# K^T of the attention heads by crossbar transpose instead of TensorE transposes, with changed loads and orders around it

## The chip, the cores and the metric

The kernel runs on one core of one Trainium2 chip. The metric is device time in microseconds (us) from the first to the last instruction of the program. The kernel before took 5017.94 us, the median of three runs (5016.48 to 5026.38).

## The reference

The kernel computes the forward output and eight gradients of a block of attention and a gated unit that are multiplied with each other:

```python
# x: 1 x 2048 x 576; 32 heads of 128; k_cache, v_cache: 1 x 32 x 2048 x 128; F = 4608
def _A_ref(x, k_cache, v_cache, wq, wo):          # attention on cached K and V
    q = (x @ wq) -> heads
    scores = einsum("bhqd,bhkd->bhqk", q, k_cache) * (128 ** -0.5)
    p = softmax(scores)
    return einsum("bhqk,bhkd->bhqd", p, v_cache) -> 2048 x 4096 @ wo
def _B_ref(x, w_gate, w_up, w_down):              # gated unit
    return (sigmoid(x @ w_gate) * (x @ w_up)) @ w_down

xn = layernorm(x)
s = _A_ref(xn, k_cache, v_cache, wq, wo)
g = silu(_B_ref(xn, w_gate, w_up, w_down))
out = x + s * g
# returned: out, and by jax.vjp with grad_out the gradients of
# x, k_cache, v_cache, wq, wo, w_gate, w_up, w_down
```

All tensors are bf16. No causal mask, no dropout: every head is a full 2048 x 2048 score matrix, forward and backward.

## The kernel before

The program goes through these stages, one after the other: LayerNorm, the gate and up products (with a guard that bounds the scores, so that the softmax needs no maximum); the down product; attention with its backward pass, head by head; then the output product with wo, the weight gradients of the gated unit, those of wq and wo, and the gradient of x.

**A head of attention** has two phases of 16 slots, one slot for each tile of 128 queries. In a slot of phase 1, `main1` makes 128 x 2048 scores in two halves, ACT applies Exp, and the slab `Pq` is transposed by a DMA transpose (`PT`). In a slot of phase 2, `main2` makes dP, turns the slab into dS in place, and has it transposed too (`dST`). Besides, TensorE works on units put into the slots: the products that read `PT` and `dST` five slots later (`tail1`, `tail2`, SKEW = 5), the K and V gradients that read the slabs as they are, and the preparation of the next head.

```python
def transpose_slab(hs, qt, name):
    T = wpt.tile([P, NT, P], bf, name=name, tag="PT")
    nc.sync.dma_start_transpose(T[:], hs.slabs[qt][:])
    return T

def s_half(hs, qt, hf):                            # reads QT and KT, both halves of the tile KQ
    ...
def main2(hs, qt, hf):
    ...                                            # dp: two matmuls of 128 x 512
    if (hf == NHF - 1) != (qt == 0 and NHF > 1 and hf in (0, NHF - 1)):
        nc.vector.scalar_tensor_tensor(Pq[:, hsl], dp[:], hs.negdelta[:, qt:qt + 1], Pq[:, hsl], op0=ALU.add, op1=ALU.mult)
    else:
        t = wt.tile([P, HW_], bf, name="t")
        nc.scalar.activation(t[:], dp[:], AF.Identity, bias=hs.negdelta[:, qt:qt + 1], scale=1.0)
        nc.vector.tensor_tensor(Pq[:, hsl], t[:], Pq[:, hsl], op=ALU.mult)
    if hf == NHF - 1:
        hs.dST[qt] = transpose_slab(hs, qt, "dST")
```

**K^T** is made from the loaded K, `Kn`, with 16 TensorE transposes into PSUM and two ACT copies out of it. For the first head this is done before attention begins, for each other head in phase 2 of the head before:

```python
def prep_kt(hs):
    KTv = hs.KT[:].rearrange("p (t q) -> p t q", q=P)
    pe_transpose_blocks(lambda j: hs.Kn[:, j, :], 0, NT, lambda g, n: KTv[:, g:g + n, :], "s")

def plan(h):
    ...                                            # pl: first slot of phase 2 of head h - 1
        for c in range(4):
            put(pl + q(c), 0, lambda c=c: load_k(hd(), c, 4))
        ...
        put(pl + q(skew + 3), NT * P, lambda: prep_kt(hd()))
```

The slots are given in program order; the framework's scheduler may place an instruction earlier on its engine.

**wo for the stage after attention** is loaded during the last head into buffers that it has finished with (`xnT`, `dsT`, a `Kn`, `Vn`, `dOn`), two heads' rows a load, each behind a small GpSimd copy that waits for a slab:

```python
def paced(slot, view, a, b):
    hs = heads[H - 1]
    nc.gpsimd.tensor_copy(view[0:1, a, 0:1], hs.slabs[slot % NT][0:1, 0:1])
    load_wo_rows(view, view_h0[id(view)], a, b)
```

In the same head SP also issues the first transposed loads of the attention output (`oT`) for that stage.

**LayerNorm turn.** In the first stage a row of x is normalised on ACT (`norm`), transposed on TensorE (`turn`) and copied out by ACT, one row per step between the ten matmuls of a gate/up step:

```python
def turn_step():
    if todo["turn"] and not (todo["norm"] and todo["norm"][0] <= todo["turn"][0] + 1):
        st = todo["turn"].pop(0)
        turn(st)
        return st
...                                                # one step:
    ready = turn_step()
    ...                                            # 5 matmuls g_ps, 5 matmuls u_ps
    put_T(ready, "s")                              # ACT copy
    nc.scalar.activation(a_row[:, cs], g_ps[:], AF.Sigmoid)
    nc.vector.tensor_tensor(h_row[:, cs], u_ps[:], a_row[:, cs], op=ALU.mult)
    ...
    ln_step(False)                                 # the next row's norm
```

Of the kernel before, what the change touches and what calls it, by code (L numbers as in the profile page):

```python
# [13 lines left out]
P = 128  # L14
# [52 lines left out]
def kernel(  # L67
# [164 lines left out]
    with tc.tile_pool(name="pa", bufs=1) as pa:  # L232
# [75 lines left out]
        with tc.tile_pool(name="a1w", bufs=1) as wp:  # L308
# [37 lines left out]
            with tc.tile_pool(name="a0", bufs=3) as sb0, tc.tile_pool(name="a0ps", bufs=2, space=PSUM) as ps0, \  # L346
# [68 lines left out]
                        norm(todo["norm"].pop(0))  # L415

                def turn_step():
                    if todo["turn"] and not (todo["norm"] and todo["norm"][0] <= todo["turn"][0] + 1):
                        st = todo["turn"].pop(0)
                        turn(st)  # L420
                        return st
# [168 lines left out]
    def attention(fast):  # L590
        with ExitStack() as es:
# [13 lines left out]
                    return ps_acc.tile([P, 4, P], f32, name="acc", tag="acc")  # L605
                return ps_acc.tile([P, 8, P], bf, name="acct", tag="acc")
            acc_box[0] = acc_alloc
            warm = stat.tile([P, 1], f32, name="warm")
            nc.scalar.activation(warm[:], eps_t[:], AF.Exp)

            def start_head(h):
                hs = heads_pre[h] if h == 0 else new_head(h)
# [83 lines left out]
            def main2(hs, qt, hf):  # L696
                Pq, hsl = hs.slabs[qt], slice(hf * HW_, (hf + 1) * HW_)
                dp = ps_big.tile([P, HW_], f32, name="dp", tag="big")
                for c in range(HW_ // CH):
                    nc.tensor.matmul(dp[:, c * CH:(c + 1) * CH], lhsT=hs.dOT[:, qt * P:(qt + 1) * P],  # L700
                                     rhs=hs.VT[:, hf * HW_ + c * CH: hf * HW_ + (c + 1) * CH], start=True, stop=True)
                if (hf == NHF - 1) != (qt == 0 and NHF > 1 and hf in (0, NHF - 1)):
                    nc.vector.scalar_tensor_tensor(Pq[:, hsl], dp[:], hs.negdelta[:, qt:qt + 1], Pq[:, hsl], op0=ALU.add, op1=ALU.mult)  # L703
                else:
                    t = wt.tile([P, HW_], bf, name="t")
                    nc.scalar.activation(t[:], dp[:], AF.Identity, bias=hs.negdelta[:, qt:qt + 1], scale=1.0)  # L706
                    nc.vector.tensor_tensor(Pq[:, hsl], t[:], Pq[:, hsl], op=ALU.mult)  # L707
                if hf == NHF - 1:
                    hs.dST[qt] = transpose_slab(hs, qt, "dST")

            def tail2(hs, qt, part):
                tail_part(hs, hs.dST[qt], hs.Kn, part)
# [69 lines left out]
            def plan(h):  # L782
                b1, b2 = 2 * NT * h, 2 * NT * h + NT
                hd = lambda: heads[h]
                pl = b2 - 2 * NT if h else None
                if h:
                    put(pl, 0, lambda: heads.__setitem__(h, start_head(h)))
                    for c in range(4):
                        put(pl + q(c), 0, lambda c=c: load_k(hd(), c, 4))
                        put(pl + q(skew + 3 + c), 0, lambda c=c: load_v(hd(), c, 4))  # L790
                    put(pl + q(4), 0, lambda: load_wo(hd()))
                    put(pl + q(5), 0, lambda: load_wq(hd()))
                    put(pl + q(skew + 3), NT * P, lambda: prep_kt(hd()))
                    put(pl + q(skew + 4), DT * P, lambda: prep_wot(hd()))
                    for sc in range(NSC):
                        put(pl + q(skew + 4 + 2 * sc), DT * CH, lambda sc=sc: prep_qt(hd(), sc))
                for qt in range(NT):
                    put(b1 + qt + skew, NT * P // 2, lambda qt=qt: tail1(hd(), qt, 0))
                    put(b1 + qt + skew, NT * P // 2, lambda qt=qt: tail1(hd(), qt, 1))
                for sc in range(NSC):  # L800
                    put(b1 + q(sc), DT * CH, lambda sc=sc: prep_dot(hd(), sc))
                    put(b1 + q(sc + 1), nb * P, lambda sc=sc: prep_don(hd(), sc))
                for qt in range(NT):
                    put(b1 + max(qt + 1, q(2 + qt // nb)), 0, lambda qt=qt: scale_don(hd(), qt))
                put(b1 + q(NSC + 2), NT * P, lambda: prep_vt(hd()))
                put(b1 + q(NTH + 2), NT * P, lambda: prep_qn(hd()))
                for qt in range(NT):
                    put(max(b1 + qt + 1, b1 + NT - 4 + qt // 2 if qt < NTH else b1 + NT + qt), 0, lambda qt=qt: scale_qn(hd(), qt))
                put(b2 + 1, 0, lambda: post1(hd()))
                parts = {}  # L810

                def first(key, rhs, lo, hi, eng, factor=1.0):
                    parts[key] = part_tile()
                    return Partial(hd(), lo, hi, rhs, parts[key], None, eng, factor)
                spread(b1 + NTH, lambda: first("v", hd().dOn, 0, NTH, "v"))
                spread(b2, lambda: Partial(hd(), NTH, NT, hd().dOn, parts["v"], out_3[0, h], None))
                spread(b2 + NTH, lambda: first("k", hd().Qn, 0, NTH, "s", SCALE))
                spread(b2 + NT, lambda: Partial(hd(), NTH, NT, hd().Qn, parts["k"], out_2[0, h], None, SCALE))
                for qt in range(NT):
                    put(b2 + qt + skew, NT * P // 2, lambda qt=qt: tail2(hd(), qt, 0))  # L820
                    put(b2 + qt + skew, NT * P // 2, lambda qt=qt: tail2(hd(), qt, 1))
# [2 lines left out]
            for h in range(H):  # L824
                plan(h)
            bl = 2 * NT * (H - 1) + NT
            dead_from = (5 - NT, 5 - NT, skew + 2, NTH + 2, -NT)
            free = [k for k in range(-NT, NT) if k < 3 - NT or (k > 3 - NT and k % 2)]
            free += [k for k in range(skew + 2, NT) if k % 2 == 0]

            def paced(slot, view, a, b):
                hs = heads[H - 1]
                nc.gpsimd.tensor_copy(view[0:1, a, 0:1], hs.slabs[slot % NT][0:1, 0:1])
                load_wo_rows(view, view_h0[id(view)], a, b)
            view_h0 = {}
            for view, h0, n, dead in sorted(wo_parts, key=lambda w: dead_from[w[3]]):
                view_h0[id(view)] = h0
                for k in range(0, n, 2):
                    at = min([f for f in free if f >= dead_from[dead]] or [NT - 1])
                    if at in free:  # L840
                        free.remove(at)
                    put(bl + at, 0, lambda at=at, view=view, k=k, n=n: paced(at, view, k, min(k + 2, n)))
            for st in range(min(2, NT)):
                put(bl + NT + skew * st, 0, lambda st=st: load_oT(oTs[st], st))
            slot = 0
# [32 lines left out]
    with late("pc") as pc, late("pcw") as pcw, late("pcf") as pcf, \  # L878
# [120 lines left out]
        dqb0 = ah0[:].rearrange("p a t f -> p (a t f)")[:, :NT * HG * P].rearrange("p (t c) -> p t c", c=HG * P)  # L999
        assert HG * P <= 2 * FB  # L1000

        def load_on(on_, hg):
            nc.gpsimd.dma_start(on_, rows_view(on2_d, hg * HG * P, HG * P))

        def load_dq(dq_, hg):
            nc.gpsimd.dma_start(dq_, rows_view(dq2_d, hg * HG * P, HG * P))

        with late("b1r", 2) as dblk, late("b1l") as ldp, late("b1t", 3) as tmpp, late("b1o", 2) as outp, \
# [5 lines left out]
            for fb in range(NFB):  # L1014
# [8 lines left out]
                    load_blk(nxt[:, 1, :, :], h_d, fb + 1)  # L1023
                du_blk = dblk.tile([P, NT, FB], bf, name="du_blk")
                dg_blk = dblk.tile([P, NT, FB], bf, name="dg_blk")
                if fb == NFB - 1:
                    if NFB % 2:
                        dqb0_late = True
                    else:
                        dqb0_late = False  # L1030
                        load_dq(dqb0, 0)
                for st in range(NT):
                    srows = slice(st * P, (st + 1) * P)
                    dh = ps.tile([P, FB], f32, name="dh")
# [10 lines left out]
                nc.gpsimd.dma_start(rows_view(dg_d, fb * FB, FB), dg_blk[:])  # L1045
                if fb == NFB - 1:
                    nc.gpsimd.dma_start(ds_all, rows_view(ds_d, 0, D))
                    load_on(onb0, 0)
                for fl in range(FB // P):
                    dwd = outp.tile([P, D], bf, name="dwd")  # L1050
                    accumulate(psa, h_blk, doB, slice(fl * P, (fl + 1) * P), dwd, "acc")
# [2 lines left out]
                for (blk_, out_, nm) in ((du_blk, out_7, "dwu"), (dg_blk, out_6, "dwg")):  # L1054
# [5 lines left out]
                        accumulate(psa, blk_, xn_all, lcols, dwT, "acc")  # L1060
                        nc.sync.dma_start_transpose(stg_[:, :, lcols], dwT[:])
                    store_T(out_, fcols, stg_)
            if dqb0_late:
                load_dq(dqb0, 0)
        pc2.release()

        pc3 = tc.alloc_tile_pool(name="pc3", bufs=1, reuse_waits="tile")
# [32 lines left out]
        with late("c2w") as wp, late("c2b") as blk, late("c2s", 2) as sb, late("c2ps", 4, space=PSUM) as ps:  # L1100
# [3 lines left out]
            for hg in range(NHG):  # L1104
                cols = slice(hg * HG * P, (hg + 1) * HG * P)
                onb, dqb = onqs[hg % 2]
                if hg + 1 < NHG:
                    load_on(onqs[(hg + 1) % 2][0], hg + 1)
                    load_dq(onqs[(hg + 1) % 2][1], hg + 1)
                dwq = dwqs[hg % 2]  # L1110
                for hl in range(HG):
                    h = hg * HG + hl
# [14 lines left out]
        with late("c4s", 2) as sb, late("c4cf") as chp, late("c4ps", 2, space=PSUM) as ps:  # L1127
# [10 lines left out]
            class Rows:  # L1138
# [24 lines left out]
                def finish(self):  # L1163
                    nj = len(ncs)
                    for sl in range(nsl):
                        st = self.sbi * nsl + sl
                        rows = slice(st * P, (st + 1) * P)
                        dxn = sb.tile([P, D], f32, name="dxn")
                        ca = sb.tile([P, nj], f32, name="ca")
                        cb = sb.tile([P, nj], f32, name="cb")  # L1170
                        junk = sb.tile([P, D], f32, name="junk")
                        for j, (n0, nn) in enumerate(ncs):
                            nc.scalar.activation(dxn[:, n0:n0 + nn], self.accs[sl][j][:, :nn], AF.Copy, accum_out=ca[:, j:j + 1])  # L1173
                            nc.vector.scalar_tensor_tensor(junk[:, n0:n0 + nn], self.accs[sl][j][:, :nn], 1.0, xn_all[:, st, n0:n0 + nn],  # L1174
                                                           op0=ALU.mult, op1=ALU.mult, accum_out=cb[:, j:j + 1])
                        cs = sb.tile([P, 2], f32, name="cs")
                        nc.vector.tensor_reduce(cs[:, 1:2], cb[:], axis=AX.X, op=ALU.add)
                        nc.vector.tensor_reduce(cs[:, 0:1], ca[:], axis=AX.X, op=ALU.add)
                        m12 = sb.tile([P, 2], f32, name="m12")
                        nc.vector.tensor_scalar(m12[:], cs[:], -1.0 / D, None, op0=ALU.mult)  # L1180
                        t = sb.tile([P, D], f32, name="t")
# [51 lines left out]
```

## Time and profile before

| what | before |
|---|---|
| device time, median of three | 5017.94 us |
| span of the profiled execution | 5024.2 us |
| TensorE matmul, busy | 4914.6 us |
| VectorE (DVE), busy | 2582.2 us |
| ScalarE (ACT), busy | 2575.9 us |
| attention, first to last slab transpose | 488.4 to 3605.9 us |
| slab transposes (PT and dST) | 512 + 512 |

A profile is one execution of the program. PE is TensorE's matmuls, PEld its weight loads, SP the engine that issues the DMA transposes, POOL (GpSimd) the one that issues most other transfers. A row of a group reads: line of the kernel, engine, operation, written tile <- read tiles, shape, count | busy us, mean ns of one | idle us of the engine just before them, and what ended most of that idle time. A matmul's mean is its pipelined duration, so the busy time over the count is what one costs in a row. A row of waits reads: who waited <- for whom: us in total, times, longest. The DMA share is the busy time of 16 DMA engines over the span; packets of different queues overlap, so it can exceed 1. In a row of the timeline the first two numbers are start and length in us, and the idle time before it stands in brackets.

### The profile page before, as it was taken

How to read it: one execution, taken by the hardware profiler on the slowest of the kernel's cores; microseconds unless marked ns; L12 is line 12 of the kernel's file. 1: busy time of each engine (PE TensorE's matmuls, PEld its weight loads, DVE VectorE, ACT ScalarE, POOL GpSimd, SP SyncE). 2: the span in 40 equal slices, each digit the busy share in tenths (PEclk: the TensorE clock that was granted, in tenths of full speed). 3: DMA queues.
4: the chain of work that ended last, by engine and by line, in shares of the span. 5: the costliest groups of instructions: out<-in, count | busy, mean ns of one | idle time of the engine just before them, and what ended most of it. 6: DMA issues, size and time to landing. Idle time of an engine off the chain costs nothing.

```text
span 5024.2 us, 128236 instructions
## 1 busy us (share of the span) xinstructions
PE 4914.6 (98%) x53584; PEld 3475.1 (69%) x54480; DVE 2582.2 (51%) x6721; ACT 2575.9 (51%) x4637; POOL 961.8 (19%) x1507
## 2 busy tenths in 40 slices
PE   9999999999999999999999999999889999999999
PEld 4445787787787788778778877877646666555554
DVE  4545666666666666666666666665425444200111
ACT  5422766766666676666667666666413333211000
POOL 3322111111111111111111111111222222211000
PEclk9999999999999999999999999999999999999999
DMA  7887999999999999999999999999996665797876
GB/s 260 273 206 167 211 213 205 206 215 212 202 214 216 201 212 208 214 208 209 215 202 213 206 213 210 209 215 203 209 196 206 195 189 183 223 264 178 171 140 121
DMA packets 2762803, 1031.39 MB, mean 205 GB/s; under 512 B 2665377, under 2 KB 2669602, under 8 KB 2762210
## 3 DMA queue, kind: packets, MB, share of 16 engines
q1 hardware_dynamic: 2659746, 699.38, 75.7%
q0 software_dynamic: 101856, 323.05, 20.0%
q8 instruction: 428, 7.01, 0.6%
q14 instruction: 165, 1.35, 0.1%
q10 hardware_dynamic: 608, 0.59, 0.0%
HBM read 175.31 MB, written 182.13 MB: 71 GB/s over the span
## 4 chain that ended last, share of the span: by engine, by line
PE 92%; DMA 3%; issue 3%; DVE 1%; ACT 0%; SPq 0%; POOL 0%; POOLq 0%; ACTq 0%; DVEq 0%
PE acc L737 18%; PE acc L677 18%; PE acc L975 13%; PE sp L630 8%; PE dp L700 7%; PE acc L1157 6%; PE acc L213 6%; PE u_ps L448 3%; PE g_ps L446 3%; PE dh L1036 3%; PE acc L531 3%; PE acct L146 2%; PE acc L945 2%; DMA dST<-Pq 1%; DMA xnT<-on_d 1%
## 5 line engine op out<-in xcount | busy, mean ns | idle before, releaser
L648 ACT ACTIVATE Pq<-sp 128x1024 bf16<-128x1024 f32 x1024 | 1048.1, 1024 | 309.7 <-PE sp L630 196.4
L737 PEld LDWEIGHTS <-Pq 128*128 128x128 bf16 x16384 | 1003.9, 98 | 244.3 <-issue 1.1
L703 DVE SCALAR_TENSOR_TENSOR Pq<-dp,negdelta,Pq 128x1024 bf16<-128x1024 f32 x512 | 655.3, 1280 | 37.7 <-PE acc L677 36.5
L706 ACT ACTIVATE t<-dp,negdelta 128x1024 bf16<-128x1024 f32 x512 | 568.1, 1116 | 178.4 <-PE dp L700 123.0
L677 PEld LDWEIGHTS <-PT 128*128 128x128 bf16 x8192 | 501.0, 98 | 128.6 <-DMA PT<-Pq 11.5
L677 PE MATMUL acc<-Vn,PT 128*128 128x128 bf16 x8192 | 547.4, 219 | 17.0 <-DMA PT<-Pq 10.1
L737 PE MATMUL acc<-dOn,Pq 128*128 128x128 bf16 x8192 | 552.3, 219 | 10.1
L677 PE MATMUL acc<-Kn,dST 128*128 128x128 bf16 x8192 | 551.3, 219 | 9.1 <-DMA dST<-Pq 5.5
L630 PE MATMUL sp<-KQ 128*128 128x512 bf16 x1762 | 547.1, 379 | 2.2 <-ACT Pq L648 2.1
L737 PE MATMUL acc<-Qn,Pq 128*128 128x128 bf16 x8192 | 540.6, 219 | 3.4
L700 PE MATMUL dp<-VT,dOT 128*128 128x512 bf16 x1728 | 540.8, 379 | 0.0
L707 DVE TENSOR_TENSOR Pq<-t,Pq 128x1024 bf16<-128x1024 bf16 x512 | 354.6, 693 | 359.7 <-ACT t L706 351.9
L677 PEld LDWEIGHTS <-dST 128*128 128x128 bf16 x8192 | 492.0, 98 | 68.2 <-DMA dST<-Pq 7.4
L718 ACT ACTIVATE dq_n<-acc,rsc 128x128 bf16<-128x128 f32 x512 | 188.4, 368 | 331.7 <-PE acc L677 329.4
L1174 DVE SCALAR_TENSOR_TENSOR junk<-acc,xn_all 128x512 f32<-128x512 f32 (+1 forms) x32 | 13.9, 453 | 635.6 <-ACT dxn L1173 635.6
L751 POOL DMA_DIRECT2D out_dram<-kvo x256 | 140.8, 550 | 999.7 <-DVE kvo L749 999.7
L671 POOL DMA_DIRECT2D on_d<-o_n x128 | 97.3, 760 | 721.4 <-DVE junk L689 374.8
L1038 DVE TENSOR_TENSOR du_blk<-dh,ah 128x256 bf16<-128x256 f32 x288 | 120.4, 419 | 195.5 <-PE dh L1036 193.4
L1173 ACT ACTIVATE dxn<-acc 128x512 f32<-128x512 f32 (+1 forms) x32 | 12.8, 407 | 396.7 <-PE acc L1157 389.2
L635 DVE TENSOR_REDUCE rs_all<-rsp 128x1 f32<-128x2 f32 x512 | 78.1, 153 | 255.7 <-ACT Pq L648 253.4
L50 DVE TENSOR_SCALAR o_n<-acc,rinv_all 128x128 bf16<-128x128 f32 x352 | 123.3, 350 | 161.5 <-PE acc L677 161.5
L648 ACT ACTIVATION_READ_ACCUMULATOR Pq<-sp 128x1 f32 x1024 | 200.5, 196 | 0.0
(213 smaller groups left out, 6977.0 us busy)
## 6 DMA issues: line engine op xcount, KB each, us to landing
out_dram<-kvo POOLq DMA_DIRECT2D x256, 128.0 KB, 4.2
ah<-a_d POOLq DMA_DIRECT2D x18, 1024.0 KB, 7.2
ah<-h_d POOLq DMA_DIRECT2D x18, 1024.0 KB, 9.4
du_d<-du_blk POOLq DMA_DIRECT2D x18, 1024.0 KB, 8.0
dg_d<-dg_blk POOLq DMA_DIRECT2D x18, 1024.0 KB, 9.7
h_d<-h_row POOLq DMA_DIRECT2D x64, 256.0 KB, 3.5
a_d<-a_row POOLq DMA_DIRECT2D x64, 256.0 KB, 3.7
x_all<-in_A_k_cache_dram SPq DMA_DIRECT2D x64, 256.0 KB, 3.8
```

Of the source, the lines that this page charges most:

```text
L213: nc.tensor.matmul(av[:, :CH], lhsT=w[:, i, :], rhs=srcT[:, i, cs], start=(i == 0), stop=(i == DT - 1))
L630: nc.tensor.matmul(sp[:, c * CH:(c + 1) * CH], lhsT=hs.QT[:, qt * P:(qt + 1) * P], rhs=hs.KT[:, hf * HW_ + c * CH: hf * HW_ + (c + 1) * CH ...
L648: nc.scalar.activation(Pq[:, hsl], sp[:], AF.Exp, scale=SCALE, accum_out=hs.rsp[:, hf:hf + 1])
L677: nc.tensor.matmul(hs.acc[:, 0, :], lhsT=T[:, kt, :], rhs=rhs[:, kt, :], start=(kt == 0), stop=(kt == NT - 1))
L700: nc.tensor.matmul(dp[:, c * CH:(c + 1) * CH], lhsT=hs.dOT[:, qt * P:(qt + 1) * P], rhs=hs.VT[:, hf * HW_ + c * CH: hf * HW_ + (c + 1) * C ...
L703: nc.vector.scalar_tensor_tensor(Pq[:, hsl], dp[:], hs.negdelta[:, qt:qt + 1], Pq[:, hsl], op0=ALU.add, op1=ALU.mult)
L706: nc.scalar.activation(t[:], dp[:], AF.Identity, bias=hs.negdelta[:, qt:qt + 1], scale=1.0)
L707: nc.vector.tensor_tensor(Pq[:, hsl], t[:], Pq[:, hsl], op=ALU.mult)
L718: nc.scalar.activation(hs.dq_n[:, qt % G4, :], hs.acc[:, 0, :], AF.Copy, scale=hs.rsc[:, qt:qt + 1])
L737: nc.tensor.matmul(self.tile[:, j, :], lhsT=self.slabs[qt][:, kt * P:(kt + 1) * P], rhs=self.rhs[:, qt, :], start=(qt == self.lo), stop=(q ...
L975: nc.tensor.matmul(accs[j][:, :nn], lhsT=lhs[:, st, cols], rhs=rhs[:, st, n0:n0 + nn], start=(st == 0), stop=(st == NT - 1))
L1157: nc.tensor.matmul(self.accs[sl][j][:, :nn], lhsT=ch[:, kk, sl * P:(sl + 1) * P], rhs=wT[:, k0 + kk, n0:n0 + nn], start=(self.k + kk == 0) ...
```

## The change

The main part: for all heads but the first, K^T comes from one DMA transpose of the loaded `Kn` straight into `KT`, on the queue that also carries the slab transposes. It is meant to take 16 transposes and two copies a head off TensorE and ACT.

```diff
+            def turn_nat(dst, src):
+                nc.sync.dma_start_transpose(dst[:].rearrange("p (t q) -> p t q", q=P), src[:].rearrange("p t d -> p (t d)"))
...
-                    put(pl + q(skew + 3), NT * P, lambda: prep_kt(hd()))
+                    put(pl + q(skew + 3), 0, lambda: turn_nat(hd().KT, hd().Kn))
```

With it come other differences. The wo rows of the last head are loaded up to four heads at a time, without the copies that hold them back:

```diff
-                for k in range(0, n, 2):
-                    at = min([f for f in free if f >= dead_from[dead]] or [NT - 1])
-                    if at in free:
-                        free.remove(at)
-                    put(bl + at, 0, lambda at=at, view=view, k=k, n=n: paced(at, view, k, min(k + 2, n)))
+                for k in range(0, n, 4):
+                    at = (1 + k // 4, q(skew + 1), q(skew + 2), q(skew + 4), q(skew + 5))[dead]
+                    put(bl + q(at), 0, lambda view=view, h0=h0, k=k, n=n: load_wo_rows(view, h0, k, min(k + 4, n)))
```

A row's turn in the first stage may follow on its own norm; the first dS slab of a head no longer takes DVE for its first half and ACT for its second; a dummy Exp at the start of attention is gone:

```diff
-                    if todo["turn"] and not (todo["norm"] and todo["norm"][0] <= todo["turn"][0] + 1):
+                    if todo["turn"] and not (todo["norm"] and todo["norm"][0] <= todo["turn"][0]):
...
-                if (hf == NHF - 1) != (qt == 0 and NHF > 1 and hf in (0, NHF - 1)):
+                if hf == NHF - 1:
...
-            warm = stat.tile([P, 1], f32, name="warm")
-            nc.scalar.activation(warm[:], eps_t[:], AF.Exp)
```

In the late stages, the dq rows of the first group of heads are loaded together with its on rows, after the gradients of the last block of the gated unit are stored, where before they were loaded ahead of that block's matmuls; and two small reduces at the end of each tile of dx become one:

```diff
-                        load_dq(dqb0, 0)
...
-                    load_on(onb0, 0)
+                    load_heads(onb0, dqb0, 0)
...
-                        nc.vector.tensor_reduce(cs[:, 1:2], cb[:], axis=AX.X, op=ALU.add)
-                        nc.vector.tensor_reduce(cs[:, 0:1], ca[:], axis=AX.X, op=ALU.add)
+                        nc.vector.tensor_reduce(cs[:], cc[:], axis=AX.X, op=ALU.add)
```

More of the change, by code (lines that the diff above doesn't have):

```diff
@@ L701, in main2 @@
                                      rhs=hs.VT[:, hf * HW_ + c * CH: hf * HW_ + (c + 1) * CH], start=True, stop=True)
-                if (hf == NHF - 1) != (qt == 0 and NHF > 1 and hf in (0, NHF - 1)):
+                if hf == NHF - 1:
                     nc.vector.scalar_tensor_tensor(Pq[:, hsl], dp[:], hs.negdelta[:, qt:qt + 1], Pq[:, hsl], op0=ALU.add, op1=ALU.mult)
+                    hs.dST[qt] = transpose_slab(hs, qt, "dST")
                 else:
@@ L707, in main2 @@
                     nc.vector.tensor_tensor(Pq[:, hsl], t[:], Pq[:, hsl], op=ALU.mult)
-                if hf == NHF - 1:
-                    hs.dST[qt] = transpose_slab(hs, qt, "dST")
             def tail2(hs, qt, part):
@@ L826, in attention @@
             bl = 2 * NT * (H - 1) + NT
[L827 to L837, printed above, removed]
-                for k in range(0, n, 2):
-                    at = min([f for f in free if f >= dead_from[dead]] or [NT - 1])
-                    if at in free:
-                        free.remove(at)
-                    put(bl + at, 0, lambda at=at, view=view, k=k, n=n: paced(at, view, k, min(k + 2, n)))
+            for view, h0, n, dead in wo_parts:
+                for k in range(0, n, 4):
+                    at = (1 + k // 4, q(skew + 1), q(skew + 2), q(skew + 4), q(skew + 5))[dead]
+                    put(bl + q(at), 0, lambda view=view, h0=h0, k=k, n=n: load_wo_rows(view, h0, k, min(k + 4, n)))
             for st in range(min(2, NT)):
@@ L1000, with load_heads @@
         assert HG * P <= 2 * FB
-        def load_on(on_, hg):
+        def load_heads(on_, dq_, hg):
             nc.gpsimd.dma_start(on_, rows_view(on2_d, hg * HG * P, HG * P))
-        def load_dq(dq_, hg):
             nc.gpsimd.dma_start(dq_, rows_view(dq2_d, hg * HG * P, HG * P))
@@ L1025 @@
                 dg_blk = dblk.tile([P, NT, FB], bf, name="dg_blk")
[L1026 to L1030, printed above, removed]
-                        load_dq(dqb0, 0)
                 for st in range(NT):
@@ L1062 @@
                     store_T(out_, fcols, stg_)
-            if dqb0_late:
-                load_dq(dqb0, 0)
         pc2.release()
@@ L1107 @@
                 if hg + 1 < NHG:
-                    load_on(onqs[(hg + 1) % 2][0], hg + 1)
-                    load_dq(onqs[(hg + 1) % 2][1], hg + 1)
+                    load_heads(*onqs[(hg + 1) % 2], hg + 1)
                 dwq = dwqs[hg % 2]
@@ L1168, in finish @@
                         dxn = sb.tile([P, D], f32, name="dxn")
-                        ca = sb.tile([P, nj], f32, name="ca")
-                        cb = sb.tile([P, nj], f32, name="cb")
+                        cc = sb.tile([P, 2, nj], f32, name="cc")
                         junk = sb.tile([P, D], f32, name="junk")
                         for j, (n0, nn) in enumerate(ncs):
-                            nc.scalar.activation(dxn[:, n0:n0 + nn], self.accs[sl][j][:, :nn], AF.Copy, accum_out=ca[:, j:j + 1])
+                            nc.scalar.activation(dxn[:, n0:n0 + nn], self.accs[sl][j][:, :nn], AF.Copy, accum_out=cc[:, 0, j:j + 1])
                             nc.vector.scalar_tensor_tensor(junk[:, n0:n0 + nn], self.accs[sl][j][:, :nn], 1.0, xn_all[:, st, n0:n0 + nn],
-                                                           op0=ALU.mult, op1=ALU.mult, accum_out=cb[:, j:j + 1])
+                                                           op0=ALU.mult, op1=ALU.mult, accum_out=cc[:, 1, j:j + 1])
                         cs = sb.tile([P, 2], f32, name="cs")
-                        nc.vector.tensor_reduce(cs[:, 1:2], cb[:], axis=AX.X, op=ALU.add)
-                        nc.vector.tensor_reduce(cs[:, 0:1], ca[:], axis=AX.X, op=ALU.add)
+                        nc.vector.tensor_reduce(cs[:], cc[:], axis=AX.X, op=ALU.add)
                         m12 = sb.tile([P, 2], f32, name="m12")
```

## The prediction

> **What bounds the kernel now.** I read the page from the top: busy time, the 40 slices, the chain that ended last. Then I cut the span into stages, and asked what the matmuls wait for.
>
> ```profile
> PE 4914.6 (98%) x53584; PEld 3475.1 (69%) x54480; DVE 2582.2 (51%) x6721; ACT 2575.9 (51%) x4637; POOL 961.8 (19%) x1507
> ...
> DMA  7887999999999999999999999999996665797876
> ...
> PE 92%; DMA 3%; issue 3%; DVE 1%; ACT 0%; SPq 0%; POOL 0%; POOLq 0%; ACTq 0%; DVEq 0%
> ```
>
> TensorE is busy 98% of the span and holds 92% of the chain. The DMA row stands at 9 all through attention, so there are two candidates for a bound. The stages (span, then busy us of each engine, clock, DMA share, GB/s) tell them apart:
>
> ```profile
> 1000.00:2000.00 1000.00, 989.13 (x12763) 796.87 (x12967) 642.61 (x1710) 685.59 (x1151) 175.84 (x287) 1.00 1.10 210
> ...
> 3450.00:3620.00 170.00, 151.49 (x1989) 123.77 (x2016) 97.82 (x213) 92.82 (x152) 36.58 (x70) 0.97 1.12 220
> 3620.00:3790.00 170.00, 153.91 (x1252) 84.22 (x1276) 51.64 (x103) 28.11 (x68) 44.51 (x78) 0.96 0.95 197
> ```
>
> In the middle of attention TensorE idles 11 of 1000 us, and going through its records I find no gap above 0.15 us between 600 and 3450 us. ACT (69%) and DVE (64%) have room. Only the last head and the start of the stage after it are loose: 18.5 and 16.1 idle us. What TensorE waits for, over the whole span:
>
> ```profile
> PE pt L376 <- ACT x_all L370: 10.5, 4, 8.5
> PE acc L677 <- DMA PT<-Pq: 10.1, 2, 7.5
> PE acc L945 <- DMA KQ<-on_d: 8.8, 2, 8.1
> PE acc L677 <- DMA dST<-Pq: 5.5, 6, 1.6
> ```
>
> These four are 35 us, the rest of the list adds 16, and none of it lies in heads 2 to 29. So an instruction taken off TensorE in a middle head is worth its full duration, as long as DMA keeps up.
>
> [...] 66 ns each for the K transposes (below), while the 219 ns in the same row is a pipelined duration. [...] after the 7.5 us wait in the last head, 16 matmuls take 1.9 us instead of 1.06. [...]
>
> **Part 1, K^T.** Two rows (busy, mean ns, idle before) give what goes:
>
> ```profile
> L146 PE MATMUL acct<-ident,Kn 128*128 128x128 bf16 x496 | 32.7, 219 | 1.6
> ...
> L40 ACT COPY KQ<-acct 128x1024 bf16<-128x1024 bf16 x62 | 59.8, 1015 | 15.8 <-PE acct L146 15.8
> ```
>
> 496 is 31 heads times 16. TensorE loses 32.7 us, 1.05 us a head, all of it in stretches without gaps: **-32.7 us** on the path. ACT loses 62 evictions, 60 us; it is not the bound, so 0. What comes in is 31 slabs on SP's transpose queue. Such a slab costs (min/median/max ns of the issuing instruction):
>
> ```profile
> L624 SPq DMA_TRANSPOSE PT<-Pq x512: 1425/2138/6610, 488.4 to 3560.5; - x171
> L624 SPq DMA_TRANSPOSE dST<-Pq x512: 1418/2252/7013, 528.2 to 3605.9; - x171
> ```
>
> Their 1024 starts run from 488.4 to 3605.9 us, so one per 3.05 us; at 2.2 us each the queue is 72% taken. In head 0, which has no K/V gradients of an earlier head beside it, 16 slabs went out in 38.4 us, 2.4 us each: DMA can do more than it is asked. A 33rd slab per head makes 72.6 us of about 97. In the built order it stands between the 15th and 16th PT slab of the head before, waits there for the last score matmul that reads the old K^T, and its data is needed a whole phase (16 slots, some 48 us) later. K itself is loaded earlier, in the first third of that phase. The 16th PT goes out about 2 us later; from end of issue to first use I measure at least 5.5 us for that slab in heads 2 to 29, and stalls begin at about 2 to 3. For the tightest slabs (PT 6 and 8, dST 7 of a head) the least is 3.5 to 3.9, and a slot of the second phase gets 1.05 us shorter. I allow **+1.5 us** for it.
>
> **Part 2, the LayerNorm turn.** A row's turn may now follow directly on its own norm, where before the next row's norm had to be issued too. The built order puts the first turn of the second half one step earlier, ahead of ten matmuls. Before, at that spot:
>
> ```profile
> 52.28 0.87 ACT L370 ACTIVATE x_all<-x_all,nbias,rstd_all 128x576 bf16<-128x576 bf16 x1 [0.48 <-DVE nbias L364]
> ...
> 53.20 0.45 PE L376 MATMUL pt<-ident,x_all 128*128 128x128 bf16 x5 [1.34 <-ACT x_all L370]
> ```
>
> The norm ends at 53.15. TensorE now meets the turn before the ten matmuls (10 x 0.216 = 2.16 us) that fill this wait: +2.2. The next turn needs a norm that ACT does only after an eviction, a 1.28 us table load and a sigmoid: by adding these rows I get it done 1.4 us after TensorE wants it. Then each step is a ring: turn 0.28, gate matmuls 1.24, sigmoid 0.5, norm 0.86, about 0.08 of semaphores, 2.96 us against 2.44 now; seven steps lose 0.5 each, 3.6. Together **+7 us**, and as no wait follows for 270 us, it reaches the end.
>
> **Part 3, wo rows in the last head.** Before, 18 loads of at most two heads (288 KB), each held back by a small GpSimd copy from a slab. After, ten loads of up to four; in the built order 26 of 32 heads' rows (147 KB each, 3.8 MB) are issued before the head's first on_d store. Before, by my count along the GpSimd queue, 22 had gone out when the last PT did. So the sum that competes with the first phase is nearly the same, but it comes as a burst at its start, and the on_d stores that the two early oT transposes wait for queue behind it, with later PT slabs in line behind these on SP. The two stalls there now (2.6 and 7.5 us) each sit right behind an oT transpose. I expect 10 to 18 us in place of 10, about 3 us less in the second phase, and again ten-odd us at half clock: **+3 us**, from -5 to +12.
>
> **Part 4, the rest.** The dq rows of the first head group go behind the store of dg, ds and on rows instead of ahead of them. From 4328 us on, 2.1 + 2.4 + 2.1 MB must land before the first use at about 4350, and 2.1 MB more before 4354; at the 340 to 390 GB/s that the stretches 4330 to 4350 show, 8.7 MB end at about 4353: 0, at worst +2. The first slab of the second phase no longer swaps ACT and DVE: in every other slab the unswapped order runs without a gap: 0. The dummy Exp goes; its 1.28 us table load sat behind TensorE's last preparing matmul and will stand at the first real Exp: 0 to +1. One reduce instead of two at the end: -0.15 twice.
>
> **Sum.** -32.7 + 1.5 + 7 + 3 + 0.5 = -20.7; 5017.9 - 20.7 = 4997 us.
>
> **Rivals.** (a) **DMA becomes the bound.** For it: share 1.10 in attention; 31 slabs at 3.05 us would be +95, making it about 5080 with the rest. Against it: 2.4 us slabs in head 0, and no TensorE gap in 28 heads, which a saturated queue would leave. (b) **The added slab is nearly hidden but slack is thin**: half a microsecond to one of stalls per head at the tight slabs eats the gain; about 5018. For it: leads of 3.5 us at the least. Against it: medians of 6 and more. (c) **The small parts cost nothing** and the K^T gain shows whole: 4985. For it: they look like scheduling details; against it: the ring in part 2 follows from measured durations. (d) **The last head jams**: the burst and a longer half-clock stretch cost 25 us: 5020.
>
> **Range and chances.** Part 3 is good for about 8 us either way, part 1's slack for 6, part 2 for 3, the measurement for 4 (three runs lie within 10 us); together about 12 to 13, with a longer tail upward. 4980 to 5017. A 2% change is 100 us: faster would need three times what is removed; slower needs rival (a) in full.
>
> **What would show it.** In the profile after: no acct<-ident,Kn row, ACT's Exp row unchanged, TensorE busy near 4882 (4914.6 - 32.7); 31 KQ<-Kn transposes of about 2.1 us; a head's period about 1 us shorter; pt L376 waits up from 10.5 to about 17; PT and dST waits in the middle heads still near zero; the wo burst and PT stalls near 3510 to 3560. I am wrong if middle heads show PT or dST waits (rival a or b), if the pt wait stays at 10 us, or if the last head loses over 30 us.

## The result and the profile after

| kernel | median us (range, runs) |
|---|---|
| before | 5019.62 (5016.48 to 5026.38, 4) |
| changed | 5046.65 (5040.28 to 5060.24, 4) |

The ratio is 1.0056, 95% interval 1.0031 to 1.0080. The change costs about 28 us; 4980 to 5017 had been predicted. The two profiled executions differ a little more: spans of 5024.2 and 5058.4 us, 34.2 apart.

The page of the changed kernel, same rows as before: busy us and share of the span, the DMA row of the slices, the shares of the chain that ended last.

```profile
PE 4900.6 (97%) x53089; PEld 3447.6 (68%) x53984; DVE 2585.6 (51%) x6705; ACT 2520.8 (50%) x4574; POOL 950.7 (19%) x1481
...
DMA  7886999999999999999999999999996665797976
...
PE 86%; DMA 7%; issue 4%; DVE 2%; ACT 1%; POOL 0%; SPq 0%; POOLq 0%; ACTq 0%; DVEq 0%
```

TensorE has 495 matmuls fewer and is only 14 us less busy, in a span that is 34 us longer. On the chain, DMA has gone from 3% to 7%. The same stretch of middle attention (span, then busy us of PE, PEld, DVE, ACT and POOL, clock, DMA share, GB/s) shows that the loss is not confined to the ends:

```profile
1000.00:2000.00 1000.00, 976.26 (x12491) 781.69 (x12693) 636.00 (x1697) 664.38 (x1126) 173.12 (x283) 1.00 1.13 214
```

By its records TensorE idled 11 us here before, now 24, and the GB/s hardly moved (210 to 214). Part of both figures is no idleness: some matmul records are missing from a profile (before has 53584, while `small_parts` below, with the same TensorE work, has all 54480). `kt_late` below has all of its 53984 and idles 1.6 us in this stretch. Busy totals are therefore compared only between profiles that lack the same share of records. The list of what TensorE waits for, over the whole span (total us, times, longest), names the transfers:

```profile
PE acc L678 <- DMA dST<-Pq: 28.9, 33, 2.2
PE pt L376 <- ACT x_all L370: 16.2, 10, 8.7
PE acc L933 <- DMA KQ<-on_d: 15.0, 3, 8.3
PE acc L678 <- DMA PT<-Pq: 13.0, 4, 6.4
PE dp L701 <- DVE Pq L704: 7.7, 32, 0.2
```

The dST wait went from 5.5 us in 6 places to 28.9 us in 33. The last row is new, and 32 is the number of heads. The slabs themselves, added one first (min/median/max ns of the issuing instruction):

```profile
L610 SPq DMA_TRANSPOSE KQ<-Kn x31: 1471/2627/3736, 534.4 to 3473.3; - x31
...
L625 SPq DMA_TRANSPOSE PT<-Pq x512: 1417/2208/8078, 496.2 to 3589.2; - x171
L625 SPq DMA_TRANSPOSE dST<-Pq x512: 1417/2371/7999, 539.9 to 3633.1; - x171
```

The new slabs take little longer than the others, 2.6 us, and the medians of the others rose by 0.07 and 0.12 us only. These are times of the issuing instruction; a dST slab lands 5.5 us after its issue in the median, before 5.3. So a slab did not become much slower in general; the loss must lie with single ones and with what waits behind them.

**Where the 34.2 us are.** I took the start of each head (the weight load of its first score matmul) from the records. The shortest distance between two heads is that of a head without a stall; what the mean has above it is waiting.

| | before | after | difference |
|---|---|---|---|
| start of head 1 | 573.7 | 581.5 | +7.8 |
| from head 1 to head 31 (30 heads) | 2922.4 | 2939.1 | +16.7 |
| shortest head / mean head | 97.36 / 97.4 | 96.79 / 98.0 | |
| last head and all that follows | 1528.0 | 1537.8 | +9.8 |

The K^T transposes are gone from the middle heads, and the shortest head is shorter, by 0.57 us. But the mean head is 0.56 us longer: gaps above 0.15 us in heads 1 to 30 add up to 35.1 us (before 1.0). About 27 of the 35 end on a dST slab, and 7 (0.24 a head) on the new DVE row. So the 16.7 us of these heads are -26.7 for K^T (0.89 a head, from the first experiment), +9.6 for 0.32 a head that the swap costs (`no_swap` below), and +33.8 left, of which dST gaps are the larger part.

**One stalled head.** SP's own queue near 1030 us (start, length), then the loads that GpSimd issues in the same time, the dST slab issued at 1034.86 (ns of the issuing instruction, and us from issue to landing), then TensorE:

```profile
1021.19 2.97 SPq L625 DMA_TRANSPOSE PT<-Pq  x1
1024.34 1.89 SPq L610 DMA_TRANSPOSE KQ<-Kn  x1
1026.32 3.24 SPq L625 DMA_TRANSPOSE PT<-Pq  x1
1029.65 23.31 SPq L625 DMA_TRANSPOSE dST<-Pq  x7
```

```profile
1034.94 1.62 POOL L178 DMA_DIRECT2D Vn<-in_A_v_cache_dram  x3 [1.09 <-PE acc L678]
1036.55 0.77 POOL L672 DMA_DIRECT2D on_d<-o_n  x1
1037.31 0.54 POOL L178 DMA_DIRECT2D Vn<-in_A_v_cache_dram  x1
```

```profile
L625 SPq DMA_TRANSPOSE dST<-Pq x1: 3330/3330/3330, 1034.9 to 1034.9; - x1
...
DMA to landing us min/median/max: 11.4/11.4/11.4
```

```profile
1046.32 1.07 PE L678 MATMUL acc<-Kn,dST 128*128 128x128 bf16 x16 [2.18 <-DMA dST<-Pq]
...
1049.48 0.62 PE L678 MATMUL acc<-Kn,dST 128*128 128x128 bf16 x8 [1.21 <-DMA dST<-Pq]
```

The K^T slab takes its 1.9 us of the queue between the last two PT slabs, and the whole row of dST slabs behind it starts that much later. Then the four loads of the next head's V (128 KB each) are issued from 1034.9 to 1037.3. The third dST slab (dST 2, counted from 0), issued at 1034.86, is in flight beside them. It lands at 1046.27, and TensorE has then stood 2.2 us for it. The next one, dST 3, keeps SP from 1038.28 for 8.00 us, and TensorE stands another 1.2 us for it. In the same head before, the three slabs beside the V loads kept SP for 3.3 to 3.7 us each, landed 6.4 to 7.8 us after their issue, and nothing waited. 15 of the 29 middle heads stall like this, nearly always at dST 1 to 4, the slabs in flight beside the V loads.

### The profile page after: what moved, and what is told of

It is laid out like the page before. It is cut to its first block, busy times and chain, and to the rows that moved or that the text cites. A ratio compares the mean times of both kernels' runs of the same rounds, so it can differ in the third digit from the quotient of the medians.

```text
span 5058.4 us, 127199 instructions
## 1 busy us (share of the span) xinstructions
PE 4900.6 (97%) x53089; PEld 3447.6 (68%) x53984; DVE 2585.6 (51%) x6705; ACT 2520.8 (50%) x4574; POOL 950.7 (19%) x1481
## 4 chain that ended last, share of the span: by engine, by line
PE 86%; DMA 7%; issue 4%; DVE 2%; ACT 1%; POOL 0%; SPq 0%; POOLq 0%; ACTq 0%; DVEq 0%
PE acc L737 17%; PE acc L678 16%; PE acc L963 13%; PE sp L631 7%; PE dp L701 6%; PE acc L1134 6%; PE acc L213 6%; DMA dST<-Pq 3%; PE g_ps L446 3%; PE u_ps L448 3%; PE dh L1016 3%; PE acc L531 3%; PE acct L146 2%; PE acc L933 1%; DMA KQ<-on_d 1%
## 5 line engine op out<-in xcount | busy, mean ns | idle before, releaser
L678 PE MATMUL acc<-Kn,dST 128*128 128x128 bf16 x8192 | 557.1, 219 | 34.1 <-DMA dST<-Pq 28.9
```

The lines of the kernel that those rows point to most:

```text
L678: nc.tensor.matmul(hs.acc[:, 0, :], lhsT=T[:, kt, :], rhs=rhs[:, kt, :], start=(kt == 0), stop=(kt == NT - 1))
```

## The experiments

**Theory**: the 33rd slab is cheap, but it uses up the lead of the slabs behind it just where the burst of V loads stretches one. **Rivals**: the transpose queue or DMA as a whole has no room for a 33rd slab, wherever it stands; or the loss is all in the small parts. Each group of four kernels below shared its runs of the kernel before (medians 5019.55, 5019.65 and 5020.01 us), and every ratio is against those.

### The K^T slab alone, and moved

`kt_alone` is the kernel before with the K^T part only:

```diff
-                    put(pl + q(skew + 3), NT * P, lambda: prep_kt(hd()))
+                    put(pl + q(skew + 3), 0, lambda: turn_nat(hd().KT, hd().Kn))
```

> The kernel before with the K^T slab as the only change. Theory Q (place in the queue): TensorE saves 16 starts of 56 ns a head, 0.89 us, 27.6 us in all; the slab pushes the last PT and the first dST slabs back by some 2.5 us, and these meet the V loads, so that waits for dST 3 and 4 of 20 to 35 us come back: 5012 to 5028 us. Theory D (DMA has no room for a 33rd slab a head, wherever it stands): about the same, 5015 to 5030. Theory S (the small parts of the change cost it all, K^T itself is a gain): 4988 to 4995, with no dST waits in the middle heads.

Measured: 5021.31 us, ratio 1.0000 (0.9989 to 1.0010). The K^T part gains nothing. The unstalled head is 96.47 us, 0.89 shorter than before; the mean head is 97.36 (before 97.41). Thirty heads should have become 26.7 us shorter and became 1.5 us shorter (2922.4 to 2920.9), so stalls cost about 25 us; gaps above 0.15 us hold 18.5 of it. The rest goes with them: set instruction by instruction beside a head without a stall, the steps that hold these gaps take 22.3 us longer (a gap counts only from the end of the matmul before it, whose tail otherwise overlaps the next one: in the stalled head above, of the changed kernel, the step from 1043.55 to 1046.32 us takes 2.77 us where it takes 0.43 without a stall, 2.34 more for a gap of 2.18), and slower matmuls after some of them add 4.5 (last section). Its waits of TensorE, over the whole span:

```profile
PE acc L683 <- DMA dST<-Pq: 18.0, 24, 2.2
PE acc L683 <- DMA PT<-Pq: 11.4, 4, 5.0
```

`kt_late` holds that slab back behind dST 10, after the V burst, by a one-element DVE copy:

```diff
+            def hold(dst, h, k):
+                nc.vector.tensor_copy(dst[0:1, 0:1], heads[h].slabs[k][0:1, 0:1])
...
+                    put(pl + q(10), 0, lambda: (hold(hd().KT, h - 1, 10), turn_nat(hd().KT, hd().Kn)))
```

> As kt_alone, but the K^T slab is held behind the eleventh dST slab of the phase (a 1-element copy on DVE from that slab into KT). Theory Q: dST slabs there have 8 us and more from issue to first use, nobody waits, period 97.37 - 0.89 = 96.48 us, total about 4992 (4987 to 4997). Theory D: the waits only move, 5015 to 5030. Theory S: 4988 to 4995 as well.

Measured: 5005.20 us, ratio 0.9970 (0.9954 to 0.9986). Gaps in heads 1 to 30 fall from 18.5 to 3.4 us and the mean head is 96.65. The median misses the expected range (4987 to 4997), with runs from 4991.86 to 5009.58; in the profiled one, 4998.0 us, thirty heads are 23.0 us shorter than before, of 26.7 possible. What the other runs lose besides is open. The same slab, the same number of slabs, another place:

```profile
PE acc L683 <- DMA dST<-Pq: 7.1, 10, 1.6
```

So the queue has room for 33 slabs a head. It is where the slab stands that costs.

### All small parts, without K^T

`small_parts` is the changed kernel with K^T back on TensorE:

```diff
-                    put(pl + q(skew + 3), 0, lambda: turn_nat(hd().KT, hd().Kn))
+                    put(pl + q(skew + 3), NT * P, lambda: prep_kt(hd()))
```

> The changed kernel with K^T back on TensorE: the small parts alone. Profile of the changed kernel adds up: start of the first stage +7.5, first dS slab of a head 0.24 x 31 = +7.4, last head and later stages +9.7. Theory Q and D: 5038 to 5046, so K^T as changed is worth about zero (within 8 us). Theory S: the small parts cost 50 or more, 5070.

Measured: 5043.53 us, ratio 1.0050 (1.0033 to 1.0067). The small parts alone make up nearly the whole loss, about 25 of 28 us. Its unstalled head is 97.68 us, 0.32 longer than before, though no K^T is touched. Its waits of TensorE show where that comes from, and that dST waits are as few as before:

```profile
PE dp L701 <- DVE Pq L704: 7.6, 32, 0.2
PE acc L678 <- DMA dST<-Pq: 3.7, 7, 1.4
```

### The slab added and nothing taken away

`extra_slab` makes K^T both ways, with the slab in the place that the change gave it, so TensorE keeps all its work:

```diff
+                    put(pl + q(skew + 3), 0, lambda: turn_nat(hd().KT, hd().Kn))
                     put(pl + q(skew + 3), NT * P, lambda: prep_kt(hd()))
```

> The kernel before with the K^T slab added at the same place, and the 16 TensorE transposes kept (they overwrite KT with the same values): the slab's cost by itself. Theory Q: dST waits of 15 to 35 us and nothing else, 5035 to 5055. Theory D: every head is longer by about 3 us, 5100 and more. Theory S: 5020 to 5025.

Measured: 5066.85 us, ratio 1.0096 (1.0079 to 1.0112), that is +47 us. In 30 heads it loses 41.8 us, with 31.8 us of gaps. The direction fits the theory, but it is more than expected (5035 to 5055) and more than the same slab costs in `kt_alone`; `extra_v_late` below comes back to this.

### The V loads moved instead

If the burst matters, moving the burst must do as well as moving the slab. `v_late` is `kt_alone` with the four V loads held back behind dST 8, 10, 12 and 14, one at a time:

```diff
-                        put(pl + q(skew + 3 + c), 0, lambda c=c: load_v(hd(), c, 4))
+                        put(pl + q((8, 10, 12, 14)[c]), 0, lambda c=c: (hold(hd().Vn[:, c * NT // 4, :], h - 1, (8, 10, 12, 14)[c]), load_v(hd(), c, 4)))
```

> kt_alone (early K^T slab), with the four V loads of the next head held behind dST slabs 8, 10, 12 and 14, where they ran beside dST 3 to 5. Theory B (the slab alone takes away slack, the V burst beside the next slabs turns it into a wait): the dST waits of kt_alone (some 17 us, on dST 1 to 4) fall below 5 us, period 96.5 us, about 4993 us, 25 below the kernel before. Theory P (the place alone, any traffic will do): waits stay at 12 to 20 us, 5012 to 5022.

Measured: 4994.53 us, ratio 0.9947 (0.9930 to 0.9964). The slab stands where it stood in `kt_alone`, and the mean head is 96.59 us. Gaps are 2.9 us in 30 heads:

```profile
PE acc L683 <- DMA PT<-Pq: 9.5, 5, 3.9
PE acc L683 <- DMA dST<-Pq: 6.0, 7, 1.7
```

`both_late` moves both, the V loads likewise and K^T behind dST 9:

```diff
+                    put(pl + q(9), 0, lambda: (hold(hd().KT, h - 1, 9), turn_nat(hd().KT, hd().Kn)))
```

> The K^T slab held behind dST 9 and the V loads behind dST 8, 10, 12, 14. Theory B: no slab lies in front of the tight ones and no burst beside them, so no middle head waits: period 96.47 us, 4988 to 4995. Theory P: as kt_late or a little worse, since the V loads now run beside the K^T slab: 4998 to 5008.

Measured: 4992.22 us, ratio 0.9940 (0.9924 to 0.9957), the fastest here and faster than both kernels of the case. The mean head is 96.58, so the second move adds nothing that the runs tell apart.

Moving the V loads might be a gain of its own. `v_late_only` does it to the kernel before, with K^T left on TensorE:

> Control: the kernel before with only the V loads held, K^T still on TensorE. Theory B: there was no wait to remove, 5020 (5016 to 5024). If the held loads bring something of their own, it is below 5015, and the gain of v_late is not K^T's alone.

Measured: 5017.96 us, ratio 0.9994 (0.9985 to 1.0003). There is no gain that can be told from zero. And `extra_v_late` is `extra_slab` with the V loads moved:

> extra_slab (K^T slab beside the kept TensorE transposes, +47 us) with the V loads held behind dST slabs 8 to 14. Theory B (a slab costs nothing by itself, only the burst behind it made it a wait): 5020 to 5026, dST waits in the middle heads under 5 us. If a 33rd slab has a cost of its own: 5035 to 5050.

Measured: 5018.06 us, ratio 0.9998 (0.9991 to 1.0005). A 33rd slab per head, with nothing taken off TensorE and in the place that the change gave it, costs nothing once the V loads are elsewhere. The waits on dST, `extra_slab` first:

```profile
PE acc L683 <- DMA dST<-Pq: 34.1, 35, 2.6
```

```profile
PE acc L683 <- DMA dST<-Pq: 4.6, 7, 1.4
```

All of the 47 us of `extra_slab` thus need the V burst. Why they are more than `kt_alone` loses, with the same slab beside the same burst, is not settled: TensorE waits longer (gaps of 31.8 us against 18.5).

### The small parts one by one

Each is put alone into the kernel before. `turn_only`, the LayerNorm condition:

```diff
-                    if todo["turn"] and not (todo["norm"] and todo["norm"][0] <= todo["turn"][0] + 1):
+                    if todo["turn"] and not (todo["norm"] and todo["norm"][0] <= todo["turn"][0]):
```

> The kernel before with only the condition of the LayerNorm turn changed. The prediction's ring: +7 us, attention begins 7 to 8 us later, 5027. If later stages swallow it: 5020.

Measured: 5028.66 us, ratio 1.0019 (1.0011 to 1.0026), about +9.5 us. Head 1 starts at 581.7 us as in the changed kernel (581.5), and the wait is the same:

```profile
PE pt L376 <- ACT x_all L370: 16.2, 12, 8.8
```

`no_swap`, the first dS slab:

```diff
-                if (hf == NHF - 1) != (qt == 0 and NHF > 1 and hf in (0, NHF - 1)):
+                if hf == NHF - 1:
```

> The kernel before with only the swap of ACT and DVE at the first dS slab taken out. From the shortest periods (97.36 before, 97.68 in small_parts) it costs 0.32 us a head, 31 or 32 times: +10 us, 5029. The prediction had it at zero: 5019.

Measured: 5031.69 us, ratio 1.0022 (1.0012 to 1.0032), about +11 us. The unstalled head is 97.68 us, as in `small_parts`: 0.32 us in each of 30 heads, 9.6 us. Its row of waits, one per head:

```profile
PE dp L700 <- DVE Pq L703: 7.7, 32, 0.3
```

The changed kernel's timeline shows why, DVE first (start, length), then TensorE:

```profile
1025.05 0.69 DVE L709 TENSOR_TENSOR Pq<-t,Pq 128x1024 bf16<-128x1024 bf16 x1
...
1025.87 1.28 DVE L704 SCALAR_TENSOR_TENSOR Pq<-dp,negdelta,Pq 128x1024 bf16<-128x1024 f32 x1
```

```profile
1027.21 0.59 PE L701 MATMUL dp<-VT,dOT 128*128 128x512 bf16 x2 [0.24 <-DVE Pq L704]
```

At the head's first dS slab ACT makes `t` of the first half and DVE multiplies it. Only then, after two more small operations, does DVE come to the second half, whose 1.28 us end at 1027.15. The next dP needs the PSUM buffer that this frees. With the swap DVE takes the first half at once and ACT the second, and the kernel before has no such wait.

`wo_only`, the loads of wo rows in the last head without their copies:

```diff
-                for k in range(0, n, 2):
...
-                    put(bl + at, 0, lambda at=at, view=view, k=k, n=n: paced(at, view, k, min(k + 2, n)))
+                for k in range(0, n, 4):
...
+                    put(bl + q(at), 0, lambda view=view, h0=h0, k=k, n=n: load_wo_rows(view, h0, k, min(k + 4, n)))
```

> The kernel before with only the wo rows loaded up to four heads at a time and not held back. Prediction: +3 us (-5 to +12), from the last head; what is left of small_parts (+24) after turn_only (+9) and no_swap (+12) says +3 as well: 5022.

Measured: 5019.03 us, ratio 1.0004 (0.9993 to 1.0015): nothing that can be told from zero.

`dq_only`, the first group's dq rows loaded after its on rows:

```diff
-                        load_dq(dqb0, 0)
...
                     load_on(onb0, 0)
+                    load_dq(dqb0, 0)
```

> The kernel before with only the dq rows of the first head group loaded behind the on rows. Prediction 0 to +2; the profile of the changed kernel has waits of 2.2 and 1.2 us there where before had 0.8: +2 to +3 us, 5022.

Measured: 5024.77 us, ratio 1.0008 (0.9998 to 1.0019), about +4 us and not clear of zero. The profile has a wait of that sort, 2.7 us:

```profile
PE acc L975 <- DMA ah<-dq_d: 2.7, 1, 2.7
```

The four come to 0.19 + 0.22 + 0.04 + 0.08 = 0.53%, some 27 us, against 0.50% for all small parts together. The dummy Exp and the joined reduces were not run alone; there is no room left for much from them.

## Why the prediction was wrong

**The bound: right.** Heads 1 to 30 had 1.0 us of gaps before, and what leaves TensorE there shortens the unstalled head. The condition "as long as DMA keeps up" did the damage.

**Part 1, -32.7 us for K^T: right in kind, too large.** The unstalled head of `kt_alone`, and of its three variants, is 0.89 us shorter, 27.6 us over 31 heads. That is 16 times 56 ns, where the prediction took the 66 ns of the busy row. Busy time over count, named above as what one costs in a row, includes the tail of each group, which the next matmul overlaps. The path pays the distance between starts, as in this row of the kernel before:

```profile
1036.24 1.06 PE L146 MATMUL acct<-ident,Kn 128*128 128x128 bf16 x16
```

The 16 transposes are busy for 1.06 us, but the next matmul starts at 1037.13, 0.89 us after the first of them.

**Part 1, +1.5 us for thin slack: this step failed.** "I measure at least 5.5 us for that slab in heads 2 to 29" looked at PT 15 alone. The slab stands ahead of all dST slabs too, and those meet the V loads. Median leads, from end of issue to first use, before and after: PT 15 7.9 to 4.8 us, dST 0 9.1 to 6.4, dST 3 7.1 to 5.0, dST 4 6.3 to 3.8, with the least at 2.3. I had set the start of stalls at 2 to 3 us of such a lead; the four PT slabs that TensorE waited for in the last head before had 2.0 to 3.2. But a slab lands some time after the end of its issue: the dST 2 above stalled with a lead of 8.1. Counted from landing, in the kernel before, dST 3 and 4 had the least time left of all 32 slabs of a head, medians of 2.5 and 2.9 us: dST 3, beside the V loads, landed 4.9 us after the end of its issue, the last two PT slabs 2.1. The changed kernel left them 0.2 and 0.8, and `v_late` 2.8 and 2.9 again (heads 2 to 29).

The prediction listed the tightest slabs with their leads under the old load, and shortened a slot by 1.05 us, but did not move the queue by a slab and then ask what else is issued in that window. The cost was about 25 us in 30 heads of `kt_alone`, nearly the whole gain. "Against it: medians of 6 and more" was no argument, since it takes only the tail: 15 of 29 heads of the changed kernel stall. Rival (b) had the mechanism, and with "half a microsecond to one" per head also the size (25 us in 30 heads are 0.8); what it had wrong was the place, other slabs, and it was passed over for the 1.5 us.

Around the 8.00 us slab the sum that the DMA engines moved was lower too: 175 GB/s in the 12 us from the first V load on, in the same place before 229. What lowered it is not shown. The 1.42 us of the shortest slab before is the issuing instruction; no slab landed in less than 3.6 us from its issue (median 5.1 for PT, 5.3 for dST), so it is no transfer time. The longest issuing instruction before took 7.0 us.

**Rival (a), DMA as the bound: refuted**, as predicted: `extra_v_late` carries the 33rd slab at 0.9998.

**Part 2, +7 us for the turn: right, mechanism and size.** The wait rose from 10.5 to 16.2 us (about 17 was foretold), attention starts 7.8 us later, and `turn_only` lost 9.5. Each piece of the ring is there in the changed kernel: the first wait is 3.50 us where it was 1.34, the second 1.29 (1.4 foretold), and turns then follow each other every 2.97 to 3.02 us (2.96 foretold).

```profile
53.40 0.45 PE L376 MATMUL pt<-ident,x_all 128*128 128x128 bf16 x5 [3.50 <-ACT x_all L370]
```

**Part 3, +3 us for wo: within its range.** `wo_only` lost 2 us, not distinguishable from 0. The wait on `KQ<-on_d` did rise in the changed kernel, from 8.8 to 15.0 us, but the last head and all that follows lost only 9.8 us, of which `dq_only` may hold 4. The granted clock stood at 0.5 for 10.2 us of the last head before (means of 0.60 in 3560 to 3570 us and 0.89 in the next ten), and in the changed kernel for 10.2 us as well (0.69 in 3550 to 3560, 0.97 in 3560 to 3570, 0.83 in 3590 to 3600).

**Part 4, 0 for the swap: this step failed as well.** "In every other slab the unswapped order runs without a gap" is true of slabs 1 to 15 of a head. At slab 0 DVE has other operations at the start of the phase to do first. Taking the swap away costs 11 us. The dq rows, "0, at worst +2", cost about 4, within the interval of 0.

**The sum with measured terms**: K^T -27.6 with +25 of stalls, turn +9.5, swap +11, dq +4, wo +2, together +24, against +28 measured; the intervals of the single terms are wider than that difference. Two terms make the error: the stalls, 25 for 1.5, and the swap, 11 for 0.

**Signs that misled.** TensorE busy was to be 4882 us and is 4900.6: a miss of 19 us. `v_late`, with as many matmul records and hardly a stall, stands at 4888.0. So 6 us of the miss are the size of the K^T term, and 13 go with the stalls and the small parts; they are not split further. "A head's period about 1 us shorter" held for the unstalled head less the swap (0.89 - 0.32 = 0.57), and failed for the mean. PT and dST waits near zero in the middle heads failed, and that had been named as the proof of rival (a) or (b).

## What to carry to other kernels

A transfer that is cheap by itself (issued in 2.6 us here) was paid for in the leads of the slabs behind it in its queue (dST 3: 7.1 to 5.0 us): move that queue by its length, find the smallest remaining lead, and look what bulk loads are issued in that window. If there is one, shift the load or the slab; here the same K^T change went from 0 to about -27 us (ratio 0.9947) by holding back four V loads. Two odd-looking exceptions of this kernel (the swap at slab 0, the `+ 1` of the turn) each kept a gap closed, worth about 11 and 9.5 us: read the timeline at exactly that spot before calling such a thing worth nothing.

## What the runs showed of the hardware

- The instruction that issues a slab of 524 KB takes 2.2 us in the median and 1.42 at the least, yet took 8.00 us beside four loads and some stores of 128 KB each. Beside the same loads it took 3.3 to 3.7 us in the kernel before. What makes the difference is not settled.
- After a wait of 2.07 us a stretch of matmuls was slow. The granted clock was 0.83 in the mean of 1830 to 1840 us, and 1.00 in the ten us before and the ten after. TensorE's timeline of the changed kernel (start, length, count, and the wait in brackets):

```profile
1832.56 0.62 PE L678 MATMUL acc<-Kn,dST 128*128 128x128 bf16 x8 [2.07 <-DMA dST<-Pq]
...
1835.20 1.82 PE L737 MATMUL acc<-Qn,Pq 128*128 128x128 bf16 x16
1836.86 1.06 PE L678 MATMUL acc<-Kn,dST 128*128 128x128 bf16 x16
```

  Sixteen matmuls take 1.82 us where the next sixteen take 1.06. So a stall can cost more than its own length. It need not: after the 2.18 us wait in the head above, 16 matmuls take 1.07 us, and the clock was 1.00 from 1040 to 1050 us. What tells the two waits apart is not shown.
- Without stalls a head's length repeats to about 0.01 us: 97.36 us before, 96.47 in four kernels with K^T on the queue, 97.68 in two without the swap. The shortest head was the sharpest measure of work on the path, sharper than any busy total.
